# First batch of a pooled attention: values by probabilities of every second head in plain float32

## The chip, the cores and the metric

The kernel runs on one core of one Trainium2 chip. Its time is the device time of one execution in microseconds (us). Before the change the median of three runs is 1350.54 us (1350.36 to 1352.05). The profiled execution took 1351.29 us; the span of its instructions is 1349.5 us, so 1.79 us lie around the span.

## The reference, cut to what matters

An attention whose queries are averaged in pairs feeds a dense layer pair with a squared relu, and that feeds a gated layer pair. All is float32 (the weights of the first layers come as float64 words, decoded on the chip).

```python
B, H, S, D = 4, 8, 1152, 64
q_pool = q.reshape(B, H, S // 2, 2, D).mean(axis=3)          # 576 queries a head
scores = q_pool @ k.T / sqrt(D)
attn = exp(scores - max(scores)); attn = attn / (sum(attn) + 1e-9)
x = (attn @ v)                                                # 4 batches, 8 heads
x = x.transpose(0, 2, 1, 3).reshape(2304, 512)
h = x @ w_in; x = (s * relu(h) ** 2 + b) @ w_out              # 512 -> 2048 -> 512
y = (sigmoid(x @ w_gate) * (x @ w_val)) @ w_out2              # 512 -> 1536 -> 512
```

## The kernel before, in words

TensorE takes its operands in a rounded float32 here (`F32R`, fp32r in the profile's rows), one pass a matmul. Where the product must stay exact, an operand is split into a rounded high part and the rounded rest, and two or three matmuls are added in PSUM. A matmul of plain `F32` operands needs no split; the trace shows it as two matmul records.

The work is described as operations with an engine (or several to choose from), a duration, what they read and write, and the buffers they hold. `Plan.order` (line 1763) then plays the engines forward with these durations: on each engine the operation with the smallest key goes that is ready and whose buffers are free. The key is a due time (from the tables `ATTENTION` and `FEED`) plus a rank plus an offset by the operation's name from the table `MOVED`. Each engine then runs its list in that order and waits for semaphores only, so an instruction that waits holds everything behind it on its engine.

The four batches are staged. Batch 0's attention runs first, almost alone; from then on the attention of batch b+1 runs between the layers of batch b, and the layers of batch 3 end the kernel. Heads go in pairs (first head j=0, second head j=1), four pairs a batch. `pair_prep` (line 2378) loads and transposes q and k and loads v. For v of a split head it loads into `vn`, copies the high part and subtracts for the low part into `vt` (lines 2404 to 2406); for a head listed in `WHOLE` it loads straight into `vt`, as plain float32. Before, `WHOLE` holds heads 0 to 3 of batch 1.

Batch 0 is computed by rows (`pair_rows`, line 2635): queries on the partitions, so maxima and sums run along the free axis. `block` multiplies 128 queries by 1152 keys in three matmul groups (line 2657), DVE takes the maxima (2664), ACT the exponentials with their sums (2671). A middle block holds the last 64 queries of both heads. `group(j, g, ...)` (line 2688) then turns the probabilities back for the product with v. For g=0 it handles 256 queries and two chunks of 128 keys at a time (five units), for g=1 320 queries and one chunk at a time (nine units): 14 units a head, 56 for the four second heads, of which 36 have 320 columns, 16 have 512 and 4 have 256. One unit is:

1. transposes of the probabilities into a PSUM bank (2702, and 2704 for the middle block);
2. the split into `g`, two ways in turn: ACT copies PSUM to `pp` (2020), POOL or ACT rounds to the high part (2015 or 2013), POOL or DVE subtracts for the low part (2023); or ACT rounds from PSUM (2020) and DVE subtracts from PSUM (2026);
3. four or two matmuls of both parts by v's low and high columns (2724), adding into one bank.

At a group's end ACT copies that bank (`r o`) and DVE adds its two halves into `x` (2026, `x<-pp`). After a pair's last group the sums are inverted and `x` is scaled (2747 to 2773). Buffers: 8 PSUM banks in all, 4 of `g`, 6 of `pp`, 6 of `st`.

SP's queue loads q, k, v and the weights in one order. ACT, DVE and POOL decode the weights beside this (lines 2043 to 2063): 11 of the 68 decodes stand before 180 us.

Of the kernel before, what the change touches and what calls it, by code (L numbers as in the profile page):

```python
# [3018 lines left out]
```

## Time and profile before

| | us |
|---|---|
| median of 3 runs | 1350.54 |
| profiled execution | 1351.29 |
| its span | 1349.5 |
| PE busy | 1313.8 (97%) |
| PE weight loads busy | 1169.8 (87%) |
| DVE busy | 1128.4 (84%) |
| ACT busy | 903.6 (67%) |
| POOL busy | 903.2 (67%) |

PE is TensorE, DVE VectorE, ACT ScalarE, POOL GpSimd, SP the queue that starts DMAs. A matmul's record covers its whole way through the array, some 0.17 us more than the time until the next may start, so records overlap: a PE that starts few matmuls can still look busy. The spacing of starts is therefore taken from runs of equal matmuls in the timeline: in a row with n of them that spans T, and with t as the length of one, the spacing is (T - t) / (n - 1).

### The profile page before, as it was taken

To read this page: it belongs to the slowest core of one execution; us is meant where nothing else is said; L and a number is where in the kernel's file an instruction comes from. 1 tells how busy PE (TensorE), PEld (TensorE's weight loads), DVE (VectorE), ACT (ScalarE), POOL (GpSimd) and SP (SyncE) were. 2 spreads that over 40 slices of the span, in tenths; PEclk is the share of its full clock that TensorE was granted. 3 is DMA by queue.
4 is the path that set the end of the run, shared out by engine and by line. 5 is a ranking of instruction groups with operands and counts; after the bars stand their busy time and mean duration, and the time that the engine had idled before them with its cause. 6 is when DMAs were issued, how large, how long until landed. Compare 5 with 4: busy or idle time off the path is not lost.

```text
span 1349.5 us, 21795 instructions
## 1 busy us (share of the span) xinstructions
PE 1313.8 (97%) x7524; PEld 1169.8 (87%) x7524; DVE 1128.4 (84%) x1848; ACT 903.6 (67%) x1919; POOL 903.2 (67%) x767
## 2 busy tenths in 40 slices
PE   7999999998999999999999999999999999999998
PEld 6888888887888898888888888888888899999997
DVE  6899887998989998889989998898978646677675
ACT  6899977667888688768777667676855364343321
POOL 4578755657789876668868877586765455446562
PEclk9999999999999999999999999999999999999999
DMA  3246325876776764445343544343333434435332
GB/s 97 54 116 216 99 90 178 280 243 222 229 259 222 265 198 163 147 160 184 131 144 137 174 165 156 148 161 142 117 143 121 159 132 159 153 120 188 125 125 47
DMA packets 102373, 214.85 MB, mean 159 GB/s; under 512 B 49756, under 2 KB 72056, under 8 KB 86136
## 3 DMA queue, kind: packets, MB, share of 16 engines
q1 hardware_dynamic: 101096, 213.18, 47.4%
q8 instruction: 59, 0.97, 0.3%
q14 instruction: 50, 0.41, 0.1%
q10 hardware_dynamic: 1168, 0.29, 0.1%
HBM read 173.02 MB, written 40.43 MB: 158 GB/s over the span
## 4 chain that ended last, share of the span: by engine, by line
PE 78%; DVE 8%; ACT 6%; POOL 3%; DMA 3%; issue 2%; DVEq 0%; POOLq 0%; ACTq 0%
PE banks L2096 11%; PE banks L2098 11%; PE banks L2097 11%; PE banks L2493 6%; PE banks L2849 4%; PE banks L2851 4%; PE banks L2850 4%; PE banks L2567 3%; PE banks L2233 3%; PE banks L2235 3%; PE banks L2234 3%; PE banks L2559 2%; PE banks L2724 2%; PE banks L2549 2%; DVE st L2026 2%
## 5 line engine op out<-in xcount | busy, mean ns | idle before, releaser
L2026 DVE TENSOR_TENSOR st<-banks,st 128x288 f32<-128x288 f32 x384 | 171.9, 450 | 29.9 <-ACT st L2020 18.2
L2096 PE MATMUL banks<-xx,w 128*128 128x512 f32 x480 | 192.9, 402 | 0.9 <-DVE raw L2059 0.8
L2097 PE MATMUL banks<-xx,w 128*128 128x512 f32 x480 | 188.8, 393 | 0.0
L2098 PE MATMUL banks<-xx,w 128*128 128x512 f32 x480 | 188.8, 393 | 0.0
L2023 POOL TENSOR_TENSOR pp<-st,pp 128x864 fp32r<-128x864 f32 x76 | 173.3, 2285 | 12.2 <-ACT pp L2013 6.0
L2020 ACT COPY st<-banks 128x288 f32<-128x288 f32 x432 | 153.6, 407 | 40.8 <-PE banks L2493 29.9
L2493 PE MATMUL banks<-qT,kT 128*128 128x288 f32 x864 | 158.6, 303 | 2.5 <-DVE y L2340 1.1
L2026 DVE TENSOR_TENSOR st<-st,banks 128x864 f32<-128x864 f32 x144 | 148.2, 1043 | 4.3 <-PE banks L2467 3.9
L2493 PEld LDWEIGHTS banks<-qT,kT 128*128 128x128 f32 x864 | 134.3, 190 | 15.1 <-DVE st L2026 1.4
L2519 ACT ACTIVATE st<-st 128x864 f32<-128x864 f32 x144 | 132.7, 935 | 19.4 <-DVE st L2026 18.3
L2098 PEld LDWEIGHTS banks<-xx,w 128*128 128x128 f32 x480 | 90.5, 189 | 20.1
L2096 PEld LDWEIGHTS banks<-xx,w 128*128 128x128 f32 x480 | 90.7, 189 | 13.2 <-DVE raw L2059 1.0
L2097 PEld LDWEIGHTS banks<-xx,w 128*128 128x128 f32 x480 | 90.9, 189 | 10.8
L2013 ACT CAST pp<-st 128x864 fp32r<-128x864 f32 x102 | 93.4, 922 | 0.8 <-PE banks L2567 0.4
L2096 PE MATMUL banks<-g,w 128*128 128x512 f32 (+2 forms) x256 | 87.4, 342 | 0.0
L2097 PE MATMUL banks<-g,w 128*128 128x256 f32 (+1 forms) x256 | 86.5, 338 | 0.0
L2098 PE MATMUL banks<-g,w 128*128 128x512 f32 (+2 forms) x256 | 86.5, 338 | 0.0
L2023 POOL TENSOR_TENSOR g<-raw,g 128x512 fp32r<-128x512 f32 (+1 forms) x31 | 54.4, 1754 | 37.4 <-ACT g L2013 18.1
L2023 POOL TENSOR_TENSOR w<-raw,w 128x512 fp32r<-128x512 f32 x55 | 75.2, 1368 | 4.9 <-ACT w L2013 4.0
L2023 POOL TENSOR_TENSOR pp<-st,st 128x864 f32<-128x864 f32 x19 | 39.6, 2083 | 43.3 <-ACT st L2519 38.8
L2023 DVE TENSOR_TENSOR pp<-st,pp 128x864 fp32r<-128x864 f32 x44 | 65.6, 1490 | 2.9 <-PE banks L2559 1.1
L2567 PE MATMUL banks<-pp,vt 128*128 128x288 f32 x360 | 67.9, 297 | 0.0
(250 smaller groups left out, 3991.8 us busy)
## 6 DMA issues: line engine op xcount, KB each, us to landing
w<-d_2g_2v SPq DMA_DIRECT2D x26, 1024.0 KB
w<-d_1u_1u SPq DMA_DIRECT2D x24, 1024.0 KB
w<-d_1d_1d SPq DMA_DIRECT2D x24, 1024.0 KB
w<-d_2d_2d SPq DMA_DIRECT2D x18, 1024.0 KB
raw<-in_moe_w_out_dram SPq DMA_DIRECT2D x28, 512.0 KB
d_2g_2v<-w SPq DMA_DIRECT2D x12, 1024.0 KB
w<-d_2g_2v SPq DMA_DIRECT2D x20, 512.0 KB
qn<-in_q_dram SPq DMA_DIRECT2D x16, 576.0 KB
```

The lines of the kernel that those rows point to most:

```text
L2013: nc.scalar.copy(out=out(), in_=in_())
L2020: act(name, n, lambda: nc.scalar.copy(out=out(), in_=in_()), r, w, rank, sbuf=False)
L2023: shared(name, n, lambda e: ENGINE[e].tensor_tensor(out=out(), in0=in0(), in1=in1(), op=op), r, w, rank, 2.25)
L2026: dve(name, n, lambda: nc.vector.tensor_tensor(out=out(), in0=in0(), in1=in1(), op=op), r, w, rank)
L2096: nc.tensor.matmul(ps(), lhsT=whi(), rhs=xhi(), start=first, stop=False)
L2097: nc.tensor.matmul((ps_lo or ps)(), lhsT=whi(), rhs=xlo(), start=False, stop=False)
L2098: nc.tensor.matmul(ps(), lhsT=wlo(), rhs=xhi(), start=False, stop=last)
L2493: nc.tensor.matmul(ps.t[:, :HQ], lhsT=kT.t[:, c], rhs=qq[:, w, hf * HQ:(hf + 1) * HQ], start=(w == 0), stop=(w == 1))
L2519: act("exp", 3 * HQ, lambda s=s: nc.scalar.activation(out=s.t[:, :3], in_=s.t[:, :3], func=AF.Exp), [], parts, AT)
L2567: nc.tensor.matmul(acc.t[:, :HQ], lhsT=vt.t[:, 3 * i + c, cols], rhs=lo.t[:, c], start=False, stop=(i == c == 2))
L2849: nc.tensor.matmul(po.t, lhsT=hi, rhs=w.t[:, 0], start=(i == 0), stop=False)
L2850: nc.tensor.matmul(po.t, lhsT=hi, rhs=w.t[:, 1], start=False, stop=False)
```

## The change

Heads 1, 3, 5 and 7 of batch 0, the second head of each pair, are added to `WHOLE`. Their v is loaded straight into `vt` as plain float32, without the copy and the subtraction. In `group` their transposed probabilities are copied once from PSUM to a `pp` buffer, by ACT or DVE as the planner chooses, and are multiplied as plain float32 by v's 64 columns, into 64 rows of the bank. ACT copies these rows straight into `x`; the addition of two halves goes. First heads stay as they were. The two tables of due times and all of `MOVED` have other numbers, so the planner's order differs from the first operations on. Of the tables two lines stand here.

```diff
-WHOLE = [(1, h) for h in range(4)]
+WHOLE = [(0, h) for h in (1, 3, 5, 7)] + [(1, h) for h in range(4)]
-ATTENTION = (0.0, 158.683, 461.124, 811.569, 1195.188)
+ATTENTION = (0.0, 141.506, 451.626, 814.023, 1176.83)
...
             n = 256 + (64 if mid else 0)
+            whole = (0, 2 * hp + j) in WHOLE
...
-                t = g_slot()
+                t = slot("pp", "pp", [P, 3 * HQ]) if whole else g_slot()
...
+                if whole:
+                    def get(e, t=t, ps=ps, m=m):
+                        if e == "ACT":
+                            nc.scalar.copy(out=t.t[:, :m], in_=ps.t[:, :m])
+                        else:
+                            nc.vector.tensor_copy(out=t.t[:, :m], in_=ps.t[:, :m])
+
+                    plan.add("r p all", {"ACT": 50 + 0.833 * m, "DVE": 70 + 1.04 * m}, 0, get, [ps], [t], AT)
+
+                    def all_pv(cs=cs, t=t):
+                        for i, c in enumerate(cs):
+                            nc.tensor.matmul(acc.t[:D, :n], lhsT=vt[j].t[:, c, D:2 * D], rhs=t.t[:, i * n:(i + 1) * n],
+                                             start=(c == 0), stop=(c == NK - 1))
+
+                    pe("r pv all", len(cs) * mm(4 * n), all_pv, [t, (vt[j], 0)], [acc], AT)
+                    continue
...
+            if whole:
+                js = slice(j * D, (j + 1) * D)
+                copy_ps("r x all", n, lambda: xt()[js, g * 256:g * 256 + n], lambda: acc.t[:D, :n], [acc], [(x, hp, g, j)], AT)
+                return
```

By the two orders the whole program has: on PE 144 matmuls by split probabilities of second heads (72 of 256 columns, 72 of 320) before, 36 and 36 in plain float32 after; on ACT 28 casts and 36 copies out of PSUM fewer, 34 copies of whole probabilities and 8 copies into `x` more; on DVE 28 subtractions from PSUM and 8 additions into `x` fewer, 22 copies of whole probabilities more; on POOL 26 casts and 30 subtractions into `g` fewer. Of v's subtractions in the whole program POOL has 10 fewer and DVE 6 more.

On PE, at the end of batch 0's last pair (second head, 256 columns; `g` holds split probabilities, `xx` and `w` are the first layer's operands, `qT` and `kT` the next batch's), this stood before:

```order
L2096 MATMUL banks_95<-xx_273_1076,w_276_1271 128x512
L2097 MATMUL banks_95<-xx_273_1076,w_276_1271 128x512
L2098 MATMUL banks_95<-xx_273_1076,w_276_1271 128x512
L2724 MATMUL banks_95<-g_263_2251,vt1_112 128x256 x4
L2724 MATMUL banks_95<-g_265_2259,vt1_112 128x256 x4
L2724 MATMUL banks_95<-g_266_2291,vt1_112 128x256 x4
L2724 MATMUL banks_95<-g_268_2299,vt1_112 128x256 x2
L2493 MATMUL banks_95<-qT_239_2137,kT_241_2196 128x288 x8
```

In the changed kernel the same place on PE reads (`pp` holds whole probabilities; lines are those of the changed file, 62 to 83 higher):

```order
L2158 MATMUL banks_95<-xx_233_906,w_236_1134 128x512
L2159 MATMUL banks_95<-xx_233_906,w_236_1134 128x512
L2160 MATMUL banks_95<-xx_233_906,w_236_1134 128x512
L2783 MATMUL banks_95<-pp_225_2057,vt1_1420_218 64x256 x2
L2568 MATMUL banks_95<-ident_60,st_397_2103 96x128 x3
L2783 MATMUL banks_95<-pp_226_2071,vt1_1420_218 64x256 x2
L2529 MATMUL banks_95<-ident_60,mc_400_2176 128x96 x3
L2783 MATMUL banks_95<-pp_227_2090,vt1_1420_218 64x256 x2
L2783 MATMUL banks_95<-pp_228_2096,vt1_1420_218 64x256 x2
L2783 MATMUL banks_95<-pp_229_2118,vt1_1420_218 64x256
```

Fourteen matmuls became nine, each with one operand buffer and half the output rows, and transposes of the next batch's maxima now stand among them.

On ACT, in the same pair where the second head's units of 320 columns are made (`sg` holds maxima and sums, `st` the exponentials), this stood before:

```order
L2020 COPY pp_249_2122<-banks_95 128x320
L2020 CAST g_250_2113<-banks_95 128x320
L2671 ACTIVATE st_260_2066,sg_208_1694<-banks_95,sg_208_1694 128x384 x3
L2443 ACTIVATE qT_239_2137<-banks_95 128x256
L2443 ACTIVATE qT_240_2138<-banks_95 128x256
L2443 ACTIVATE qT_239_2137<-banks_95 128x256
L2671 ACTIVATE st_261_2119,sg_208_1694<-banks_95,sg_208_1694 128x384 x2
L2020 COPY pp_252_2182<-banks_95 128x320
L2020 CAST g_253_2178<-banks_95 128x320
```

In the changed kernel ACT has there:

```order
L2082 COPY pp_205_1949<-banks_95 128x320
L2775 COPY pp_214_1955<-banks_95 128x320
L2775 COPY pp_215_1961<-banks_95 128x320
L2775 COPY pp_216_1967<-banks_95 128x320
L2775 COPY pp_217_1972<-banks_95 128x320
L2775 COPY pp_218_1977<-banks_95 128x320
L2775 COPY pp_219_1982<-banks_95 128x320
L2733 ACTIVATE st_223_1937,sg_177_1638<-banks_95,sg_177_1638 128x384 x3
L2733 ACTIVATE st_224_1990,sg_177_1638<-banks_95,sg_177_1638 128x384 x3
L2505 ACTIVATE qT_208_2006<-banks_95 128x256
```

The copies and casts in turn became six copies in a row, which take six `pp` buffers, and the exponentials stand behind them.

## Rows read from the trace of the kernel before

**Rows 1.** Windows: length, busy PE, PEld, DVE, ACT, POOL, granted clock, DMA, GB/s
```profile
0.00:20.00 20.00, 12.04 (x51) 9.74 (x52) 12.71 (x30) 10.86 (x30) 7.20 (x15) 1.00 0.54 148
20.00:180.00 160.00, 149.95 (x1052) 136.35 (x1051) 141.70 (x320) 143.11 (x417) 115.30 (x145) 0.99 0.36 108
180.00:500.00 320.00, 312.53 (x1825) 273.13 (x1824) 288.90 (x530) 242.21 (x479) 231.63 (x226) 0.99 0.69 226
500.00:1000.00 500.00, 494.38 (x2740) 426.42 (x2739) 441.55 (x636) 363.71 (x731) 363.26 (x247) 1.00 0.44 150
```

**Rows 2.** Groups of PE's matmuls, 0 to 180 us
```profile
L2702 PE MATMUL banks<-ident,st 128*128 128x128 f32 x288 | 50.6, 282 | 3.2 <-DVE kT L2026 1.6 <-ACT pp L2020 0.6 <-DVE x L2026 0.4
L2657 PE MATMUL banks<-kT,qT 128*128 128x384 f32 x192 | 48.6, 369 | 3.3 <-DVE g L2026 1.0 <-DVE sg L2667 0.9 <-ACT st L2671 0.7
L2724 PE MATMUL banks<-g,vt 128*128 128x320 f32 x144 | 29.2, 322 | 1.8 <-DVE kT L2026 1.8
L2704 PE MATMUL banks<-ident,st 128*128 128x64 f32 x144 | 24.8, 255 | 0.0
L2724 PE MATMUL banks<-g,vt 128*128 128x256 f32 x144 | 22.3, 288 | 0.8 <-DVE g L2026 0.6 <-POOL g L2023 0.2
```

**Rows 3.** Timeline of PE: start, length, runs of equal matmuls
```profile
64.41 1.21 PE L2657 MATMUL banks<-kT,qT 128*128 128x384 f32 x6
...
130.03 1.04 PE L2702 MATMUL banks<-ident,st 128*128 128x128 f32 x8
...
146.78 1.10 PE L2724 MATMUL banks<-g,vt 128*128 128x256 f32 x8
...
163.20 1.42 PE L2724 MATMUL banks<-g,vt 128*128 128x320 f32 x8
...
200.11 1.62 PE L2549 MATMUL banks<-st,vt 128*128 128x288 f32 x6
...
645.14 0.39 PE L2096 MATMUL banks<-xx,w 128*128 128x512 f32 x1
645.37 0.40 PE L2097 MATMUL banks<-xx,w 128*128 128x512 f32 x1
```

**Rows 4.** The plain float32 matmuls of batch 1, as a group
```profile
L2549 PE MATMUL banks<-st,vt 128*128 128x288 f32 x144 | 38.5, 407 | 0.5 <-ACT st L2519 0.3
```

**Rows 5.** Groups of PE's matmuls, 500 to 1000 us
```profile
L2096 PE MATMUL banks<-xx,w 128*128 128x512 f32 x265 | 106.0, 400 | 0.0
...
L2493 PE MATMUL banks<-qT,kT 128*128 128x288 f32 x500 | 89.9, 298 | 0.1
L2096 PE MATMUL banks<-g,w 128*128 128x512 f32 x128 | 50.7, 396 | 0.0
...
...
L2567 PE MATMUL banks<-pp,vt 128*128 128x288 f32 x252 | 47.5, 297 | 0.0
```

**Rows 6.** Groups of ACT, DVE and POOL that make and split probabilities, 0 to 180 us
```profile
L2020 ACT COPY pp<-banks 128x320 f32<-128x320 f32 x44 | 18.8, 441 | 6.1 <-PE banks L2704 4.3 <-PE banks L2724 0.9 <-POOL xx L2023 0.6
...
L2026 DVE TENSOR_TENSOR g<-banks,g 128x320 fp32r<-128x320 f32 x36 | 17.4, 484 | 4.2 <-ACT g L2020 3.7
...
L2052 DVE TENSOR_SCALAR banks<-raw 128x512 uint32<-128x512 uint32 x11 | 7.4, 684 | 0.1
...
L2023 POOL TENSOR_TENSOR g<-pp,g 128x320 fp32r<-128x320 f32 x31 | 27.1, 876 | 3.1 <-ACT g L2013 1.2
...
L2015 POOL TENSOR_SCALAR g<-pp 128x320 fp32r<-128x320 f32 x33 | 16.0, 487 | 23.3 <-ACT pp L2020 20.8 <-issue 2.2
```

**Rows 7.** Waits of PE's queue for the split, 20 to 180 us: total, times, longest
```profile
PEld banks L2724 <- POOL g L2023: 3.1, 5, 2.0
...
PEld banks L2657 <- DVE g L2026: 1.6, 2, 1.1
```

**Rows 8.** Windows: a stretch at a lower granted clock
```profile
120.00:125.00 5.00, 3.21 (x23) 2.79 (x21) 4.59 (x10) 4.59 (x14) 4.75 (x7) 0.92 0.88 203
125.00:130.00 5.00, 5.00 (x34) 4.99 (x34) 4.23 (x14) 4.11 (x13) 4.10 (x7) 0.74 0.56 150
```

More of the change, by code (lines that the diff above doesn't have):

```diff
@@ new lines @@
+    "g lo :1": -624.213,
+    "g lo :1 1": -587.005,
+    "g lo :1 2": -736.919,
+    "g lo :1 3": -317.86,
+    "w load :1": 8.74,
+    "w load :1 1": -22.206,
+    "w load :1 2": 16.638,
+    "w load :1 3": 38.371,
+    "w top :1": -110.713,
+    "w top :1 0": -131.577,
+    "w top :1 1": -164.894,
+    "w top :1 2": -245.257,
+    "w scale :1": 96.148,
+    "w scale :1 0": -3.73,
+    "w scale :1 1": -235.138,
+    "w scale :1 3": 75.471,
+    "w low :1": 19.303,
+    "w low :1 0": 22.056,
+    "w low :1 1": -3.699,
@@ new lines @@
+    "w keep :1 1": 869.269,
+    "w keep :1 3": 498.251,
+    "ff down :1": -600.214,
+    "ff down :1 0": -465.814,
+    "ff down :1 1": -107.207,
+    "ff down :1 3": -53.711,
+    "ff y add :1": 146.753,
+    "ff y add :1 0": 29.181,
+    "ff y add :1 2": 190.059,
+    "ff y add :1 3": 171.806,
+    "column sum :1": 57.83,
+    "column sum :1 1": 53.611,
+    "column sum :1 2": 41.358,
+    "column sum :1 3": 37.225,
+    "bias :1": 17.433,
+    "bias :1 3": 21.995,
+    "y bias :1": -0.85,
@@ new lines @@
+    "h lo :1": -158.518,
+    "h lo :1 0": -133.518,
+    "h lo :1 2": -124.896,
+    "h lo :1 3": -90.807,
+    "w load :2": -24.975,
+    "w load :2 1": -22.925,
+    "w load :2 2": 58.903,
+    "w load :2 3": 22.318,
+    "w top :2": 80.612,
+    "w top :2 0": 134.907,
+    "w top :2 1": 218.068,
+    "w top :2 3": 201.198,
+    "w scale :2": 41.411,
+    "w scale :2 1": -148.93,
+    "w scale :2 2": 181.077,
+    "w scale :2 3": -219.6,
+    "w low :2": -40.146,
+    "w low :2 0": -1.826,
+    "w low :2 2": 97.295,
@@ new lines @@
+    "down 2 :2": -168.386,
+    "down 2 :2 0": 10.346,
+    "down 2 :2 1": -6.571,
+    "down 2 :2 2": -187.646,
+    "out :2": -8.384,
+    "out :2 0": -8.138,
+    "w load :3": 168.825,
+    "w load :3 0": -36.531,
+    "w load :3 2": -253.414,
+    "w load :3 3": -59.871,
+    "w top :3": 48.639,
+    "w top :3 1": 29.343,
+    "w top :3 2": 45.677,
+    "w top :3 3": 160.293,
+    "w scale :3": 24.221,
+    "w scale :3 0": -87.852,
+    "w scale :3 2": -188.209,
+    "w scale :3 3": -157.584,
@@ L926 @@
+    "w lo :3 1": -68.671,
+    "w lo :3 2": -34.004,
+    "w keep :3": 369.214,
+    "w keep :3 0": 114.032,
+    "w keep :3 2": 149.92,
+    "w keep :3 3": 390.672,
+    "down 2 :3": 9.803,
+    "down 2 :3 0": 15.338,
+    "down 2 :3 2": -311.876,
+    "down 2 :3 3": -109.951,
+    "out add :3": 10.34,
+    "out add :3 1": -33.597,
+    "out add :3 2": 26.511,
+    "out add :3 3": -12.594,
+    "p2 xx up :3": 281.512,
+    "p2 xx up :3 0": -97.163,
     "p2 xx up :3 1": 3.827,
     "p2 xx up :3 2": 21.574,
-    "gate :3": 0.463,
@@ new lines @@
+    "out store :3 0": 41.464,
+    "out store :3 3": 52.021,
+    "qk @0": 40.127,
+    "qk @0 1": -21.099,
+    "qk @0 2": -184.437,
+    "qk @0 3": -23.193,
+    "s copy @0": 8.959,
+    "s max @0": -16.368,
+    "s max @0 0": -188.17,
+    "s max @0 1": -65.497,
+    "s max @0 3": -159.561,
+    "max T @0": -192.521,
+    "max T @0 0": 174.768,
+    "max T @0 1": -148.037,
+    "max T @0 2": -259.244,
+    "max @0": -80.712,
+    "max @0 1": 86.267,
+    "max @0 2": -151.52,
+    "max @0 3": 89.838,
@@ L1669 @@
[L1669 to L1683 removed]
+    "qk @1 2": -28.613,
+    "s copy @1": 120.385,
+    "s copy @1 0": 127.998,
+    "s copy @1 1": -4.138,
@@ new lines @@
+    "s copy @1 2": 6.364,
+    "s max @1": 121.767,
+    "s max @1 0": -101.619,
+    "s max @1 1": 31.012,
+    "s max @1 3": -98.237,
+    "max T @1": -63.755,
+    "max T @1 0": 239.184,
+    "max T @1 2": -43.605,
+    "max T @1 3": -130.542,
+    "max @1": 210.27,
+    "max @1 0": 506.456,
+    "max @1 1": 58.353,
+    "max @1 3": 433.273,
+    "max rows @1": -351.52,
+    "max rows @1 1": -178.99,
+    "max rows @1 2": -636.598,
+    "max rows @1 3": -913.163,
+    "s - max @1": 184.599,
@@ new lines @@
+    "s - max @1 1": 620.011,
+    "s - max @1 2": 199.794,
+    "s - max @1 3": 471.631,
+    "exp @1": 776.939,
+    "exp @1 1": 320.705,
+    "exp @1 2": 692.83,
+    "exp @1 3": 662.865,
+    "pv whole @1": 3.899,
+    "pv whole @1 0": 43.739,
+    "pv whole @1 2": -187.488,
+    "pv whole @1 3": -60.627,
+    "sums @1": -14.447,
+    "sums @1 1": -16.459,
+    "sums @1 3": -12.914,
+    "x @1": 16.622,
+    "x @1 0": -33.843,
+    "x @1 2": -44.603,
+    "x @1 3": -20.148,
+    "sums out @1": -45.981,
@@ new lines @@
+    "qk @3 1": -18.925,
+    "qk @3 2": -20.672,
+    "s copy @3": 185.616,
+    "s copy @3 0": -17.68,
+    "s copy @3 1": 22.231,
+    "s copy @3 2": 13.996,
+    "s max @3": -105.437,
+    "s max @3 0": -81.914,
+    "s max @3 1": 58.588,
+    "s max @3 3": -153.681,
+    "max T @3": -209.929,
+    "max T @3 0": 167.066,
+    "max T @3 1": -449.527,
+    "max T @3 3": -270.095,
+    "max @3": 185.726,
+    "max @3 0": 636.758,
+    "max @3 1": -38.346,
+    "max @3 3": 52.347,
+    "max rows @3": -206.994,
@@ new lines @@
+    "W whole :0 2": 94.598,
+    "T :0": -138.639,
+    "T :0 0": -42.904,
+    "T :0 1": -6.118,
+    "T :0 2": -185.319,
+    "T hi :0": -64.726,
+    "T hi :0 0": -42.028,
+    "T hi :0 1": -51.013,
+    "T hi :0 3": -174.535,
+    "T lo :0": -104.467,
+    "T lo :0 1": -41.899,
+    "T lo :0 2": -8.069,
+    "T lo :0 3": -190.338,
+    "ff B11 :0": -324.026,
+    "ff B11 :0 1": 30.958,
+    "ff B11 :0 2": -73.555,
+    "ff B11 :0 3": -91.592,
+    "ff first :0": 116.928,
+    "ff first :0 0": 115.025,
@@ new lines @@
+    "ff first :0 1": 147.057,
+    "ff first :0 2": 114.901,
+    "ff B21 :0": 1.537,
+    "ff B21 :0 1": 6.874,
+    "ff B21 :0 2": -9.635,
+    "ff sum :0": 56.28,
+    "ff sum :0 0": 140.984,
+    "ff sum :0 1": -43.588,
+    "ff sum :0 3": -121.057,
+    "ff T2 :0": -6.432,
+    "ff T2 :0 0": 2.73,
+    "ff T2 :0 1": 15.28,
+    "ff T3 :0": 129.013,
+    "ff T3 :0 1": -12.458,
+    "ff T3 :0 2": 1.182,
+    "ff T3 :0 3": -3.906,
+    "ff T1 :0": -232.69,
+    "ff T1 :0 0": -22.045,
+    "ff T1 :0 2": 59.462,
@@ new lines @@
+    "T hi :1 1": -63.623,
+    "T hi :1 3": -28.537,
+    "T lo :1": -8.219,
+    "T lo :1 1": 18.364,
+    "T lo :1 2": 39.4,
+    "T lo :1 3": -2.489,
+    "ff B11 :1": 59.047,
+    "ff B11 :1 0": -92.935,
+    "ff B11 :1 2": -179.601,
+    "ff B11 :1 3": -44.011,
+    "ff first :1": -124.656,
+    "ff first :1 0": -29.186,
+    "ff first :1 2": -106.684,
+    "ff B21 :1": -6.226,
+    "ff B21 :1 0": -243.865,
+    "ff B21 :1 1": 266.78,
+    "ff B21 :1 3": -136.039,
+    "ff sum :1": -0.361,
@@ new lines @@
+    "p2 yy up :2": -8.946,
+    "p2 yy up :2 0": 3.521,
+    "p2 yy up :2 2": -36.376,
+    "p2 yy up :2 3": 6.841,
+    "w fetch half :2": 152.976,
+    "w fetch half :2 0": 62.714,
+    "w fetch half :2 2": 49.076,
+    "w fetch half :2 3": 36.2,
+    "W whole :2": 8.657,
+    "W whole :2 0": 12.261,
+    "W whole :2 2": 23.104,
+    "W whole :2 3": 24.027,
+    "T :2": 11.539,
+    "T :2 0": 43.356,
+    "T :2 1": 17.758,
+    "T :2 2": 75.039,
+    "T hi :2": -126.17,
+    "T hi :2 1": -76.122,
@@ new lines @@
+    "p2 B22 :2 1": -3.966,
+    "p2 B22 :2 2": -59.609,
+    "p2 B22 :2 3": 0.917,
+    "w fetch half :3": -34.138,
+    "w fetch half :3 3": -56.471,
+    "W whole :3": -146.044,
+    "W whole :3 0": -36.372,
+    "W whole :3 1": -82.563,
+    "W whole :3 2": -73.665,
+    "T :3": 113.224,
+    "T :3 0": 182.314,
+    "T :3 1": 106.707,
+    "T :3 3": 93.283,
+    "T hi :3": 14.634,
+    "T lo :3": -63.79,
+    "T lo :3 0": -169.7,
+    "T lo :3 2": -42.968,
+    "T lo :3 3": -92.861,
+    "p2 B11 :3": 26.063,
@@ new lines @@
+    "p2 B11 :3 0": -2.227,
+    "p2 B11 :3 2": -169.531,
+    "p2 B11 :3 3": -109.677,
+    "p2 first :3": 6.382,
+    "p2 first :3 0": -7.627,
+    "p2 first :3 2": -24.913,
+    "p2 B21 :3": 40.279,
+    "p2 B21 :3 0": 54.855,
+    "p2 B21 :3 1": 89.639,
+    "p2 B21 :3 3": 19.198,
+    "p2 sum :3": 1.531,
+    "p2 T2 :3": 25.492,
+    "p2 T2 :3 0": 61.285,
+    "p2 T2 :3 2": 107.917,
+    "p2 T2 :3 3": 50.546,
+    "p2 T3 :3": -24.195,
+    "p2 T3 :3 1": 20.122,
+    "p2 T3 :3 2": 2.001,
+    "p2 T3 :3 3": 3.615,
```

1645 lines of the change are left out of this document (680 added, 965 removed), and 1402 rows, old and new, of the table MOVED.

## The prediction, made blind

> **What bounds the kernel now.** I read the windows first, with one cut where batch 0's attention ends, then PE's groups and its timeline, then the groups of the other engines and the waits. In the windows the reader is to see two regimes [rows 1]. From 500 to 1000 us PE is busy 494 of 500 us (98.9%), DVE 88%, ACT and POOL 73%. From 20 to 180 us, batch 0's attention, PE is busy 150 of 160 us (94%), DVE 141.7 (88.6%), ACT 143.1 (89.4%) and POOL 115.3 (72%). Records of matmuls overlap, so I weigh PE by spacing. Runs of equal matmuls give (1.21 - 0.369) / 5 = 0.168 us for 384 columns, (1.04 - 0.282) / 7 = 0.108 for a transpose, (1.10 - 0.288) / 7 = 0.116 for 256 columns, (1.42 - 0.322) / 7 = 0.157 for 320, and 0.23 between the starts of two of 512 [rows 2, 3]. A plain float32 matmul of 288 columns is two records, each (1.62 - 0.407) / 5 = 0.243 [rows 3, 4].
>
> Up to 180 us PE issues 1103 matmuls (51 in the first 20 us and 1052 in the 160 behind them [rows 1]). By groups: 288 x 0.108 = 31.1, 192 x 0.168 = 32.3, 144 x 0.157 = 22.6, 144 x 0.116 = 16.7; the 144 records of 64 columns scaled from the plain float32 ones, 0.243 x 64 / 288 = 0.054, give 7.8 [rows 2]. The other 191, transposes and 384-column ones, I put at 0.13 (between 0.108 and 0.168), 25 us. The sum is 135; less 51 x 0.13 = 7 in the first 20 us, 129 us of work stand in the 160 us stretch: 81%. The same reckoning from 500 to 1000 us: 3 x (265 + 128) matmuls of 512 columns at 0.23 are 271, 500 + 2 x 252 of 288 columns (two groups of 252, one shown) at 0.137 (between 256 and 320) are 137, and 557 others at about 0.15 are 84: 492 of 500, 98% [rows 1, 5]. So in batch 0's attention PE has about 31 us to spare while DVE and ACT are as full as they get anywhere; later PE itself is the bound.
>
> **The change part by part.** *PE, added.* Second heads have 72 matmuls of 256 and 72 of 320 columns, half of the two groups [rows 2]: 72 x 0.116 + 72 x 0.157 = 19.7 us go. In come 36 + 36 plain float32 ones, two records each: 72 x 0.243 x 256 / 288 + 72 x 0.243 x 320 / 288 = 15.6 + 19.4 = 35.0. Net +15.3 us of PE work, all before about 180 us. That the new ones fill only 64 output rows no row prices; from below it could save half of 35, from above nothing. I take nothing, since columns alone set the spacing of every row here.
>
> *ACT.* 28 casts and 36 copies go, 34 + 8 copies come: 22 fewer x 0.441 = 9.7 us less [rows 6], 143 becomes 133.
>
> *DVE.* 28 subtractions from PSUM go, 28 x 0.484 = 13.6; 8 additions go, at the same 0.484 about 3.9; 22 copies from PSUM come. No row shows this copy; the subtraction of the same 320 columns from PSUM (0.484) bounds it near by, the 512-column operation (0.684) from above, and nothing below about 0.4 is likely. I take 0.484, 10.6 us; at 0.684 it would be 15.0. If all 6 v subtractions that DVE has more (576 columns, so at least 0.684) fall here, 4.1. Net between -7 and +1.6; I take -4 us [rows 6].
>
> *POOL.* 26 roundings x 0.487 and 30 subtractions x 0.876 into `g` go: 39 us less [rows 6].
>
> *Waits.* PE's named waits for the split are 3.1 + 1.6 = 4.7 us for both heads, so some 2.4 go [rows 7]. A new hold comes: a whole unit keeps its `pp` buffer until PE has multiplied it (2 x 0.27 = 0.54 us for 320 columns), and six copies in a row on ACT take all six. The next copy would then wait for PE, and behind it on ACT stand exponentials, which the next transposes wait for. POOL needs the same buffers for first heads. The load of a second head's v now waits on SP until PE has left that `vt` buffer, with weight loads queued behind. I cost it at nothing, as the next pair's first head (its matmuls by v alone are 9.8 us / 2 = 4.9 us by the terms above) stands between; without that cover each of three pairs would wait for one load.
>
> *What it comes to.* PE's work in the stretch becomes 129 + 15.3 = 144 us. The stretch ends unchanged if PE is filled to 144 / 160 = 90%. If DVE stays at 88.6%, its 4 us less are worth 4 / 0.886 = 4.5 us; ACT (133 of 155, 86%) and POOL no longer bind. PE would have to be filled to 144 / 155.5 = 92.6%, above the 81% of now and under the 98% seen later with DVE equally full. I take 5 us off, since ACT's 10 us less also frees DVE of its waits. Behind the stretch PE has the same work as before and hardly a gap, so the end moves by what the stretch's end moves. The sum against the profiled execution: 1349.5 + 1.8 - 5 = 1346.3; it lies 0.75 above the median, so 1345.5.
>
> A rule speaks against this. The trace over the whole span has PE's weight loads as the busiest record there is to judge PE by, 87% against DVE's 84%; in this stretch the order is turned, 136.35 of 160 (85%) against 88.6% and 89.4% [rows 1]. The Trainium skill ("Perfetto Trace Analysis", Identifying the Most-Contended Engine) says to judge TensorE by its weight loads, not by its matmuls, and to spare the fullest engine first. Taken over the span, that rule makes all 15.3 us arrive at the end, which is rival D; taken by regime, which the page also asks for, it agrees with the sum above.
>
> From 125 to 130 us the granted clock was 0.74 of 2.4 GHz, part of it at 1.2 GHz, after 5 us in which PE was busy only 3.21 [rows 8]. The Trainium skill ("TensorE: Matmul & The Clock Gate", What's actually happening) has activity hold the gate open and idleness close it. By it a fuller PE would get back up to 0.08 x 5 + 0.26 x 5 = 1.7 us here and the sum would be 1343.8; I leave it out, since the dip can as well move.
>
> **The rivals.**
> *A, slower: buffers held by PE.* Place: second heads' copies on ACT and DVE, above. Most of PE's idle time before its groups is put down to k's low parts, maxima and exponentials [rows 2], which the change does not touch, so the gaps may stay gaps and PE's new work come on top. It decides when PE's fill stays under 90%. At 87%, about midway between 81% and the 92.6% that I count on, the stretch is 144 / 0.87 = 166 us, 6 longer: 1356.5. Against it: fewer steps lie between transposes and products, and banks come free after one copy instead of two readers.
> *B, no change: given back.* From 180 to 500 us DVE is 90% busy and DMA 0.69 [rows 1], with 57 of 68 decodes still to come. Layers that could start 5 us sooner then wait for weights, and the end stands: 1350.5. For it: that stretch is the fullest for DMA. Against: the decodes' engines lose work too.
> *C, much faster.* ACT, DVE and POOL together lose some 53 us; PE fills to 98% as later: 144 / 0.98 = 147 us, 13 shorter, 1337.5. Against it: the chain from scores to products still crosses three engines in each block.
> *D, slower by all of it.* PE bounds everywhere, and 15.3 us arrive: 1365.8. For it: PE's 94% in the stretch; against: 31 us of spacing unfilled there.
>
> **How the numbers follow.** What a measurement here can tell from no change is about 0.2%, 2.7 us. Forecast 0.38 (1341 to 1348 is its own range, from a DVE copy of 0.4 to 0.684 us and a fill of 91 to 95%), C 0.16, B 0.22, A 0.16, D 0.08. Faster is forecast and C, 0.54; the same is B, 0.22; slower is A and D, 0.24. The range from 1336 to 1359 leaves out D, a little of A and a little of C, some 0.17.
>
> **What would show it.** Right: line 2783's records have a spacing of 0.21 to 0.22 and 0.27; PE's last work of batch 0's attention, just before 180 us so far, comes at about 175; DVE stays near 88% up to there, ACT falls to 86%, POOL under 55%. Wrong: ACT or DVE copies of line 2775 and 2777 that wait for PE (A); the same early end, but the first layers' matmuls idle on weights (B); PE work over 98% up to 170 us and an end before 170 (C); an end of the stretch after 190 us (D). If second records start closer than 0.2 us, plain float32 is cheaper than batch 1's rows say and the gain is larger.

## The result, and the profile after

The changed kernel takes 1363.88 us (median of 4 runs, 1361.23 to 1364.63) against 1350.45 for the kernel before in the same comparison: a ratio of 1.0093, 95% interval 1.007 to 1.0116. It is slower by about 12.6 us; the forecast was 1345.5, 5 us faster. The profiled execution of the changed kernel took 1361.23 us with a span of 1359.4, 9.9 us more than the span before.

The windows of the changed kernel, with the columns of [rows 1], and one cut more at 200 us:

```profile
0.00:20.00 20.00, 13.03 (x53) 10.60 (x54) 13.29 (x32) 10.31 (x30) 6.47 (x15) 1.00 0.60 162
20.00:180.00 160.00, 156.22 (x995) 124.91 (x993) 128.88 (x295) 125.59 (x370) 71.03 (x89) 1.00 0.33 102
20.00:192.00 172.00, 168.22 (x1058) 132.91 (x1056) 138.13 (x312) 132.44 (x387) 71.66 (x90) 1.00 0.32 99
180.00:200.00 20.00, 20.00 (x112) 14.98 (x111) 14.63 (x28) 12.45 (x31) 2.54 (x3) 1.00 0.20 45
500.00:1000.00 500.00, 494.77 (x2760) 428.41 (x2761) 451.39 (x647) 365.14 (x732) 365.89 (x248) 1.00 0.44 148
```

The transposes of batch 0's inverted sums, which close a pair, start at 58.3, 96.9, 141.5 and 179.8 us before and at 56.4, 100.3, 145.2 and 191.9 after. So batch 0's attention ends 12.1 us later, and the row from 20 to 192 us is the one to lay beside 20 to 180 in [rows 1]: PE is busy 98% of it instead of 94%, while DVE (80%), ACT (77%) and POOL (42%) have fallen from 89, 89 and 72%. From 500 us on PE is as full as before.

PE's groups from 0 to 192 us, with the columns of [rows 2] (line 2783 is the new plain float32 product, 2803 the split one):

```profile
L2719 PE MATMUL banks<-kT,qT 128*128 128x384 f32 x192 | 46.7, 367 | 0.3 <-ACT st L2733 0.2
L2783 PE MATMUL banks<-pp,vt 128*64 128x320 f32 x72 | 24.7, 450 | 0.0
...
L2783 PE MATMUL banks<-pp,vt 128*64 128x256 f32 x72 | 17.3, 385 | 0.0
L2803 PE MATMUL banks<-g,vt 128*128 128x320 f32 x72 | 15.2, 324 | 0.4 <-POOL g L2085 0.4
L2803 PE MATMUL banks<-g,vt 128*128 128x256 f32 x72 | 10.5, 283 | 0.0
```

Before, PE idled 3.3 us ahead of the score matmuls [rows 2]; now it is 0.3. PE is nearly never seen idle, and a busy share can no longer tell what it loses. The timeline of PE at two places, with the columns of [rows 3], does:

```profile
56.95 1.58 PE L2719 MATMUL banks<-kT,qT 128*128 128x384 f32 x6
58.46 4.10 PE L2783 MATMUL banks<-pp,vt 128*64 128x256 f32 x18
62.49 0.80 PE L2719 MATMUL banks<-kT,qm 128*128 128x384 f32 x3
...
85.42 1.34 PE L2719 MATMUL banks<-kT,qT 128*128 128x384 f32 x6
86.69 1.29 PE L2783 MATMUL banks<-pp,vt 128*64 128x320 f32 x4
87.91 0.44 PE L2765 MATMUL banks<-ident,st 128*128 128x128 f32 x2
```

From the second record of a run of equal matmuls on, the spacing is as forecast: 0.216 us for 256 columns and 0.269 for 320 in the median. At the ends of a run it isn't. The four records of the second one above start at 86.69, 87.01, 87.27 and 87.54, so the first gap is 0.320 us; the transpose follows at 87.91, 0.363 us later instead of 0.269. About 95 ns are lost on entering line 2783, some 50 on its first record and again about 95 on leaving it, and no row calls that idle. Only the weight loads' waits hint at it (same columns as [rows 7], 20 to 192 us):

```profile
PEld banks L2783 <- issue: 3.7, 19, 0.3
PEld banks L2765 <- issue: 2.5, 5, 0.5
```

The granted clock's fall at 120 to 130 us [rows 8] is absent in this execution, with a fuller PE:

```profile
120.00:125.00 5.00, 4.65 (x37) 4.34 (x36) 4.02 (x10) 4.42 (x13) 3.33 (x5) 1.00 0.71 281
125.00:130.00 5.00, 5.00 (x32) 3.33 (x31) 4.58 (x11) 4.04 (x12) 3.49 (x5) 1.00 0.42 116
```

That does not hold for the kernel as such. The profiled execution has a mean granted clock of 0.999 over its span; the three others of the changed kernel have 0.995 to 0.996 and take 2.5 to 3.4 us longer. Where the clock fell in them no trace shows. So some of the 12.6 us can be clock: at 0.998 to 0.999 the kernel with 128 rows below is 7.6 us ahead by the spans, against 8.5 by the ratios.

### The profile page after: what moved, and what is told of

Read it like the earlier page. It is cut to its first block, busy times and chain, and to the rows that moved or that the text cites. A ratio compares the mean times of both kernels' runs of the same rounds, so it can differ in the third digit from the quotient of the medians.

```text
span 1359.4 us, 21680 instructions
## 1 busy us (share of the span) xinstructions
PE 1329.3 (98%) x7524; PEld 1162.6 (86%) x7524; DVE 1130.8 (83%) x1833; ACT 895.7 (66%) x1895; POOL 859.7 (63%) x706
## 5 line engine op out<-in xcount | busy, mean ns | idle before, releaser
L2088 DVE TENSOR_TENSOR st<-banks,st 128x288 f32<-128x288 f32 x384 | 171.5, 449 | 24.6 <-ACT st L2082 14.2
L2085 POOL TENSOR_TENSOR pp<-st,pp 128x864 fp32r<-128x864 f32 x71 | 158.4, 2237 | 13.3 <-ACT pp L2075 7.8
L2075 ACT CAST pp<-st 128x864 fp32r<-128x864 f32 x107 | 98.0, 921 | 0.7 <-PE banks L2629 0.4
L2085 POOL TENSOR_TENSOR pp<-st,st 128x864 f32<-128x864 f32 x24 | 50.6, 2108 | 67.4 <-ACT st L2581 46.6
L2085 DVE TENSOR_TENSOR pp<-st,pp 128x864 fp32r<-128x864 f32 x49 | 78.6, 1605 | 8.5 <-ACT pp L2075 6.1
L2733 ACT ACTIVATE st<-banks,sg 128x384 f32<-128x384 f32 x108 | 62.7, 601 | 17.1 <-DVE sg L2729 16.6
```

What stands on the lines that cost most here:

```text
L2075: nc.scalar.copy(out=out(), in_=in_())
L2085: shared(name, n, lambda e: ENGINE[e].tensor_tensor(out=out(), in0=in0(), in1=in1(), op=op), r, w, rank, 2.25)
L2088: dve(name, n, lambda: nc.vector.tensor_tensor(out=out(), in0=in0(), in1=in1(), op=op), r, w, rank)
L2733: act("r exp", 384 + 224, lambda c=c, ps=ps: nc.scalar.activation(out=p.t[:, c * 384:(c + 1) * 384], in_=ps.t[:, :384], func=AF.Exp, bias= ...
```

## The experiments

Theory 1, made after the result: PE, not ACT and DVE, sets the stretch once it gets more work; the plain float32 columns (15.3 us) and the switches to and from the 64-row matmuls (about 7) arrive, less what fits into gaps. Rivals: that copies wait for `pp` buffers which PE holds; that the re-tuned tables cost the time; and the prediction's own, that ACT and DVE are the bound. Differences in us below are (ratio - 1) x 1350.5, with the interval of the ratio.

### The 64 output rows

`e3_cols128`:

```diff
-nc.tensor.matmul(acc.t[:D, :n], lhsT=vt[j].t[:, c, D:2 * D], rhs=t.t[:, i * n:(i + 1) * n],
+nc.tensor.matmul(acc.t[:, :n], lhsT=vt[j].t[:, c, D:], rhs=t.t[:, i * n:(i + 1) * n],
```

> The changed kernel with one thing altered: the plain float32 products of the second heads take v's 64 columns and the 64 columns of ones beside them as weights, so that all 128 output rows are filled, as batch 1's plain float32 products do. The order on every engine is that of the changed kernel. Theory 1 (TensorE bounds batch 0's attention, and 64-row plain float32 matmuls pay some 95 ns at each switch to or from another kind, about 7 us in sum): 1355 to 1359 us. Rival (TensorE waits for buffers that whole probabilities hold, or for a chain through ACT and DVE): no change against the changed kernel's 1363.9, 1362 to 1366. Rival (the re-tuned tables cost the time): the same, 1362 to 1366.

Measured: ratio 1.003 (1.0018 to 1.0041), +4.1 us against before, so 8.5 us better than the change; the spans, 1351.8 and 1359.4, differ by 7.6. The same places in its timeline:

```profile
55.17 1.58 PE L2719 MATMUL banks<-kT,qT 128*128 128x384 f32 x6
56.60 4.05 PE L2783 MATMUL banks<-pp,vt 128*128 128x256 f32 x18
60.29 0.88 PE L2719 MATMUL banks<-kT,qm 128*128 128x384 f32 x3
...
83.73 0.86 PE L2719 MATMUL banks<-kT,qT 128*128 128x384 f32 x4
84.43 1.24 PE L2783 MATMUL banks<-pp,vt 128*128 128x320 f32 x4
85.50 0.38 PE L2765 MATMUL banks<-ident,st 128*128 128x128 f32 x2
```

Two products (four records) now take 85.50 - 84.43 = 1.07 us up to the next kind, against 87.91 - 86.69 = 1.22. From the records of both traces, 20 to 192 us (median ns between two starts):

```
switch                                   64 rows   128 rows   times
scores (384 columns) -> line 2783            268        172      10
transpose (128 columns) -> line 2783         202        109       6
transpose (64 columns) -> line 2783          205        112       6
line 2783, 320 columns -> transpose          363        269      15
line 2783, 320 columns -> q, k transpose     363        269       5
line 2783, 320 columns, first -> second      320        272      25
line 2783, 256 columns, first -> second      267        219       8
transposes behind line 2783, first -> second 165        109      15
```

Each switch costs 93 to 96 ns with 64 rows. Two more gaps grow, by about 50 to 55 ns each: behind the first record of a run, and behind the first record of the kind that follows. The gaps between are the same in both kernels. From the last record before a run to the second record behind it, 64 rows cost 291 ns in the median of 33 runs, 8.5 us in their sum. Batch 0's attention, with the same columns in the same order, ends at 184.9 us instead of 191.9: 7.0 of the 7.6 us are there.

`e5_pe_64` and `e5_pe_128` do the same in the kernel before, with its order and its splits untouched:

```diff
-                    for w in range(2):
+                    for w in range(j, 2):      # once for second heads
                         for i, c in enumerate(cs):
+                            if j:      # e5_pe_128: acc.t[:, :n] and columns :2 * D
+                                nc.tensor.matmul(acc.t[:D, :n], lhsT=vt[j].t[:, c, D:2 * D].bitcast(F32),
+                                                 rhs=part(t, 1)[:, i * n:(i + 1) * n].bitcast(F32), ...)
+                                continue
 ...   # e5_pe_64 also: the copy and the addition at a group's end read the 64 rows
```

> The kernel before, with its order, its tables and its splits as they were, but each second head's chunk multiplied once in plain float32 with 64 output rows (of the low part alone, so x of these heads is wrong) instead of twice in one pass: only TensorE's side of the change. Theory 1 (TensorE bounds here already): 15.3 us of columns and up to 7 us of switches arrive less a few us of gaps, 1364 to 1373 us. The prediction's theory (31 us to spare on TensorE beside full ACT and DVE): hidden, 1350 to 1355. Rival (tables): about the kernel before, 1350 to 1355.

> As the run with TensorE's side of the change alone (order, tables, splits of the kernel before; each second head's chunk multiplied once, in plain float32, by the low part; x of these heads is wrong), but with all 128 output rows filled: the added columns (15.3 us) without the switches of 64 rows. Theory 1, now with a threshold (TensorE has some 10 us to spare, since 9.9 us less work moved nothing, and beyond that each us arrives): 15.3 - 10 = 5 us slower than before, 1353 to 1357. Rival (every us of added TensorE work arrives): 1361 to 1366. The prediction's theory (31 us to spare): 1349 to 1352.

Measured: 1.011 (1.0096 to 1.0124), +14.9 us, with 64 rows; 1.0053 (1.0039 to 1.0067), +7.2, with 128. Their spans, 1362.3 and 1354.7, again differ by 7.6; a run of 64 rows costs 292 ns more in the median of 25. So PE's side alone is enough for the whole loss of the change, and the price of the 64 rows is shown in two orders.

### Tables and buffers

`e4_relief` keeps the change's order and tables but gives PE its old work back:

```diff
-nc.tensor.matmul(acc.t[:D, :n], lhsT=vt[j].t[:, c, D:2 * D], rhs=..., start=(c == 0), ...)
+for w in range(2):   # pp rounded, a constant as weights
+    nc.tensor.matmul(acc.t[:, :n], lhsT=cw.to_broadcast([P, P]), rhs=..., start=(c == 0 and w == 0), ...)
```

> The changed kernel, with the second heads' products given back their former cost on TensorE: the probabilities are copied once as before, but rounded, and multiplied twice in one pass each by a constant 128-column weight, so x of these heads is not the product with v. ACT, DVE and POOL stay relieved as in the change; order and tables are the changed kernel's. Theory 1 (the added TensorE work is the whole loss): not slower than the kernel before, 1343 to 1351 us. Rival (the tables cost the time, not the arithmetic): 1360 to 1365. Rival (pp buffers held until TensorE has multiplied them): part of the loss stays, since a unit is still held 0.32 us instead of 0.54: 1355 to 1360.

Measured: 1.0022 (1.0012 to 1.0032), +3.0: 9.6 us of the change's 12.6 go with PE's work alone. The rest was missed by theory 1: with all the relief and PE as before, this is still not faster than before. `e9_full_oldorder` below, the change's arithmetic with 128 rows in the old order, has +5.0 against +4.1 for `e3_cols128` in the new: for that arithmetic the new tables are no loss. With the relief alone they are one: `e8_relief_oldorder` below has -3.0 in the old order against +3.0 here, though this run takes more work from the other engines. So the rest belongs, as far as these runs tell, to an order made for other operations. Three runs meant to part tables from arithmetic let the planner order anew with the old tables:

```diff
 # e1_128_oldtables: e3_cols128    e4b_relief_oldtables: e4_relief, product planned as 2 * mm(n)
 # e6a_half_old: e3_cols128 with heads (3, 7) in place of (1, 3, 5, 7)
-ATTENTION = (0.0, 141.506, ...)   # FEED and MOVED likewise
+ATTENTION = (0.0, 158.683, ...)
```

> The changed kernel with 128 output rows, and with the due times and offsets of the kernel before in place of its own. Theory 1 (arithmetic costs the time, the tables only fit it to the order): not faster than the same with the new tables (1354.0), 1353 to 1362. Rival (the new tables cost several us): faster, 1345 to 1350.

> The relief of ACT, DVE and POOL alone, as before with a constant 128-column weight in two passes (x of the second heads is not the product with v), but with the tables of the kernel before and with the planner's duration for these products set to that of two passes, so that the order is not laid out for slow products. The prediction's theory (ACT and DVE bound batch 0's attention, TensorE has room): 5 to 13 us faster, 1337 to 1346. Rival (neither alone bounds it; the chain from scores to products and TensorE's order do): within 3 us of before, 1348 to 1353.

> Half the dose: only heads 3 and 7 of batch 0 in plain float32, with 128 output rows, tables of the kernel before. TensorE gets 7.7 us more, ACT, DVE and POOL about half of the relief. Threshold theory (some 10 us of TensorE work fit into the gaps): no slower than before, 1346 to 1351. Rival (added work arrives in proportion, 3.8 us for the whole dose): 1351 to 1354. Rival (each us arrives): 1357.

Measured: 1.022, 1.0178 and 1.0142, 19 to 30 us slower. All three missed what either theory expected: the old tables fit one set of operations, and these three got a poor order with them (in the first, the second pair takes 62.2 us instead of 38.7). They tell nothing of the arithmetic; from here on every kernel keeps the order of before, instruction by instruction.

### What bounded the stretch before

`e7_less_pe`, less for PE alone:

```diff
-                    for w in range(2):
+                    for w in range(j, 2):
```

> The kernel before, with the second heads' high products left out (72 matmuls of 256 and 72 of 320 columns, half of what they multiply; x of these heads is only the low part's product): 9.9 us less work for TensorE by spacing, everything else and the order unchanged. Theory 1 (TensorE bounds batch 0's attention): 6 to 10 us faster, 1340 to 1345 us. The prediction's theory (ACT and DVE bound it, TensorE has 31 us to spare): within 2 us of the kernel before, 1348 to 1352.

Measured: 0.9997 (0.9985 to 1.0009), no change. Theory 1 as first stated falls for the kernel before: there PE is not the bound. What is left out is the high part's product; the low part's, which waits for the subtraction, stays. In the profile the 9.9 us came back as waits and as a lower clock (its waits of PE's queue, then its windows):

```profile
PEld banks L2724 <- POOL g L2023: 6.3, 11, 2.0
```

```profile
40.00:45.00 5.00, 3.51 (x19) 3.11 (x20) 4.47 (x9) 4.20 (x12) 0.51 (x2) 0.74 0.56 121
45.00:50.00 5.00, 4.95 (x39) 4.67 (x39) 3.54 (x10) 4.80 (x16) 1.75 (x3) 0.92 0.04 6
...
120.00:125.00 5.00, 2.71 (x19) 2.20 (x18) 4.61 (x10) 4.86 (x14) 4.67 (x8) 0.93 0.86 216
125.00:130.00 5.00, 5.00 (x26) 4.96 (x26) 4.23 (x14) 3.84 (x12) 4.09 (x7) 0.50 0.52 138
130.00:135.00 5.00, 4.91 (x30) 4.01 (x29) 4.86 (x10) 4.12 (x10) 3.77 (x4) 0.89 0.84 300
```

The wait for POOL's split was 3.1 us [rows 7] and is 6.3. The clock misses 0.26 + 0.08 + 0.07 + 0.50 + 0.11 of five us each, 5.1 us, where before it missed 1.7 [rows 8]. Over all executions the difference is smaller: the clock of the whole span is 0.9965 here in the mean of 11 and 0.9984 for the kernel before in the mean of 20 beside them, some 2.5 us of 1350.

`e8_relief_oldorder` and `e11_dve_relief` relieve the others and leave PE its work:

```diff
 # units of second heads, one copy in place of the split; PE multiplies the high part twice
+act("r p", ..., nc.scalar.copy(out=part(t, 0)[:, :m], in_=ps.t[:, :m]))           # first way, both
+dve("r pT lo", ..., nc.vector.tensor_copy(out=part(t, 0)[:, :m], in_=ps.t[:, :m])) # second way, e8
+act("r pT hi", ..., nc.scalar.copy(out=part(t, 0)[:, :m], in_=ps.t[:, :m]))        # second way, e11
```

> The relief alone at the order of the kernel before, kept instruction by instruction: the second heads' probabilities are rounded out of PSUM once (by ACT or by DVE in turn), the other copy, the rounding and both kinds of subtraction are left out, and TensorE multiplies the high part twice, so it does the same work as before (x of these heads lacks the low parts). ACT loses about 12 us, POOL about 42, DVE's subtractions become copies. The prediction's theory (ACT and DVE bound batch 0's attention, TensorE is free 31 us): 5 to 13 us faster, 1337 to 1345. Two limits side by side (TensorE with its chain as near as ACT and DVE): within 4 us of before, 1346 to 1351.

> The relief at the order of the kernel before with DVE's part in place of ACT's: every unit of a second head is rounded out of PSUM once by ACT, DVE's 28 subtractions (13.6 us) and POOL's work on these heads are left out, ACT keeps its amount, TensorE multiplies the high part twice (x of these heads lacks the low parts). If DVE bounds batch 0's attention: 6 to 13 us faster than before, 1337 to 1344. If several engines in turn bound it (relief of ACT and POOL gave 1348.1): within 4 us of before, 1346 to 1350.

Measured: 0.9978 (0.9966 to 0.999), -3.0 us, and 0.997 (0.9958 to 0.9981), -4.1. Row 20 to 180 us of e8, then of e11:

```profile
20.00:180.00 160.00, 150.37 (x1067) 136.68 (x1066) 141.29 (x321) 131.35 (x386) 80.43 (x99) 1.00 0.37 110
```

```profile
20.00:180.00 160.00, 150.70 (x1067) 138.06 (x1066) 130.27 (x293) 141.19 (x414) 80.16 (x99) 0.99 0.36 110
```

Against [rows 1], e8 frees ACT of 11.8 us and POOL of 35, e11 frees DVE of 11.4 and POOL of 35. Neither brings more than 4.1 us: even if all of that were DVE's doing, a us less of its work is worth 0.36 us of time, not 1 / 0.886 = 1.13.

`e10_both` and `e14_dve_and_pe` are these two with one product a chunk:

```diff
-                    for w in range(2):
+                    for w in range(2 - easy):     # easy: second heads of batch 0
```

> The relief at the order of the kernel before, and in addition only one product a chunk (the high part by both parts of v; x of the second heads lacks the low part of the probabilities): TensorE has 9.9 us less, ACT 12 and POOL 42 less. Two limits side by side: only both together pay, 6 to 12 us faster than before, 1338 to 1344, though less TensorE work alone gave nothing (1349.8). If ACT and DVE alone bound: the same as the relief alone, within 2 us of that run. If the order or another chain bounds: within 3 us of before.

> The order of the kernel before; each unit of a second head is rounded out of PSUM once by ACT, and multiplied once, by the low and high parts of v: DVE loses 28 subtractions (13.6 us), POOL its work on these heads, TensorE 9.9 us (x of the second heads lacks the low part of the probabilities). If DVE and TensorE are limits side by side: 8 to 13 us faster than before, 1337 to 1342. If the chain from scores through ACT to products holds the stretch: no faster than with DVE relieved alone (1346.2), 1344 to 1348; if the granted clock falls more often with the emptier TensorE, up to 3 us of it are given back.

Measured: 0.9989 (0.9977 to 1.0002), -1.5 us, and 0.9959 (0.9941 to 0.9977), -5.5; the second is the fastest of all kernels here, but with the shortened product. Theory 1, by now "two limits side by side", misses both: the intervals of e10 and e8, and of e14 and e11, overlap. Row and largest waits of PE's queue in e14:

```profile
20.00:180.00 160.00, 145.59 (x986) 131.47 (x984) 130.57 (x292) 140.37 (x412) 79.89 (x98) 0.96 0.36 110
```

```profile
PEld banks L2703 <- DVE kT L2026: 4.2, 3, 2.0
PEld banks L2657 <- ACT st L2671: 3.4, 7, 1.1
```

PE now waits for banks that DVE's split of the next pair's k and ACT's exponentials still read (in the kernel before 2.3 and 1.2 us in that view), and its clock is down to 0.96 over 160 us. In the order of before no single engine holds the stretch. That steps which hand over to each other hold it is argued, not shown, and which chain of them stays open. ACT and DVE were relieved together in the new order alone (`e4_relief`), so that these two bound it side by side is not ruled out.

### The dose

`e9_full_oldorder` and `e12_full_act` are the whole change with 128 rows in the old order, with e8's and e11's copies; `e13_third_pair` (head 5, ACT's copies) and `e13_half` (heads 3 and 7, e8's copies) are parts of it:

```diff
+nc.tensor.matmul(acc.t[:, :n], lhsT=vt[j].t[:, c, D:].bitcast(F32),        # e13: :2 * D, v split
+                 rhs=part(t, 0)[:, i * n:(i + 1) * n].bitcast(F32), start=(c == 0), stop=(c == NK - 1))
```

> The whole change's arithmetic with 128 output rows at the order of the kernel before: as the run before it, but unrounded, with v copied unrounded and one plain float32 product a chunk; the reference's result is computed. TensorE gets the 15.3 us of columns, the relief as there. Threshold theory with no worth of the relief: 1353 to 1358, as TensorE's side alone with 128 rows (1356.6). If the relief makes room: 1344 to 1350. The prediction's theory: 1340 to 1346.

> As the whole arithmetic at the order of before (plain float32, 128 output rows, the reference's result), with every unit copied by ACT, so that DVE loses its 28 subtractions instead of ACT its casts. If TensorE bounds once its 15.3 us are added: as with the other relief, 1354 to 1358. If DVE was what kept TensorE's gaps open: 1343 to 1350.

> Only head 5 of batch 0 in plain float32 probabilities, at the order of before: copied once by ACT, multiplied by the low and high parts of v side by side (128 output rows, parts added as before; the reference's result). 3.8 us more TensorE work, in the pair that has its largest gaps, its only fall of the granted clock (1.7 us) and a DVE that is 96 to 98% busy. Threshold theory: hidden, and the clock may come back: 1347 to 1350. In proportion (5.5 of 15.3): 1351 to 1352.

> Heads 3 and 7 of batch 0 in the same way, at the order of before, with the copies by ACT and DVE in turn: 7.7 us more TensorE work, half of the relief. Threshold theory (some 10 us fit): 1348 to 1351. In proportion: 1352 to 1353. Each us arrives: 1357.

Measured, with what PE gets by spacing:

```
kernel            PE work   relief        time against before (interval)
e7_less_pe           -9.9   none          -0.4 (-2.0 to +1.2)
e13_third_pair       +3.8   head 5         0.1 (-1.2 to +1.4)
e13_half             +7.7   heads 3, 7    +6.1 (+3.9 to +8.2)
e5_pe_128           +15.3   none          +7.2 (+5.3 to +9.0)
e9_full_oldorder    +15.3   ACT, POOL     +5.0 (+3.1 to +7.0)
e12_full_act        +15.3   DVE, POOL     +7.0 (+4.7 to +9.2)
e3_cols128          +15.3   all, new order +4.1 (+2.4 to +5.5)
```

15.3 us of columns cost 4 to 7 us, whoever is relieved, so 8 to 11 fit in. They don't fit evenly: head 5's 3.8 us vanish in the pair with the largest gaps, heads 3 and 7 pay 3.9 to 8.2 us for their 7.7, against the threshold theory's 1348 to 1351. Part of that can be clock: the six executions go from 1353.8 us at a mean clock of 1.000 to 1359.1 at 0.995. In the profile the clock fell where it did not before, in the first pair, whose instructions and their order are the same in both:

```profile
40.00:45.00 5.00, 3.66 (x24) 3.16 (x24) 4.47 (x9) 4.35 (x14) 0.98 (x3) 0.85 0.53 121
45.00:50.00 5.00, 5.00 (x35) 4.94 (x35) 3.04 (x9) 3.73 (x13) 1.26 (x2) 0.81 0.00 0
```

In the kernel before:

```profile
40.00:45.00 5.00, 3.66 (x29) 3.12 (x27) 4.66 (x11) 4.81 (x14) 0.99 (x3) 1.00 0.59 121
45.00:50.00 5.00, 5.00 (x42) 4.92 (x41) 4.20 (x13) 4.74 (x16) 1.42 (x4) 1.00 0.10 20
```

0.15 + 0.19 of five us each are 1.7 us; the edit begins behind this pair, so they are not its work. Such falls come and go between executions of one kernel too: the executions of the kernel before have mean clocks from 0.995 to 1.000.

## Why the prediction was wrong

*The work, right.* Spacing 0.21 to 0.22 and 0.27 (0.216 and 0.269, but for the first gap of a run); ACT -9.7, DVE -4, POOL -39 against -10.7, -3.6 and -43.6 (143.1 to 132.4, 141.7 to 138.1, 115.3 to 71.7 up to the stretch's end). DVE's copy, which no row showed, was taken at 0.484 and is 0.483 us, as the groups of DVE and ACT in the changed kernel, 20 to 180 us, show:

```profile
L2777 DVE COPY pp<-banks 128x320 f32<-128x320 f32 x17 | 7.6, 483 | 2.4 <-PE banks L2767 2.2
```

```profile
L2775 ACT COPY pp<-banks 128x320 f32<-128x320 f32 x19 | 7.8, 430 | 4.1 <-PE banks L2767 2.9 <-issue 0.7 <-DVE banks L2117 0.3
```

(columns as in [rows 6]; the second row is ACT's copy).

*The 64 rows, wrong by 8 us.* "I take nothing, since columns alone set the spacing of every row here." Every row read was a run of equal matmuls, and inside a run that holds. What 64 rows cost stands at its ends, 291 ns a run: 7.6 us of span in two orders, 8.5 and 7.7 by the ratios. "From above nothing" was no bound. The trace before could mislead, since it has one-pass matmuls of 64 rows between others, at 0.13 us either way:

```profile
367.79 0.29 PE L2562 MATMUL banks<-pp,vt 128*64 128x288 f32 x1
367.92 0.29 PE L2561 MATMUL banks<-pp,vt 128*128 128x288 f32 x1
368.05 0.29 PE L2562 MATMUL banks<-pp,vt 128*64 128x288 f32 x1
```

The Trainium skill ("TensorEngine Tiling (Array Packing)", Key Properties) says that a change of the tiling mode drains TensorE, and under Available Configurations it lists 128x64 apart from 128x128. The stops of 93 to 96 ns agree, the one-pass rows do not; which instructions change the mode no run here shows. The sentence should have been a rival with a price.

*The fill, wrong by 9.4 us.* "PE would have to be filled to 144 / 155.5 = 92.6%." With 128 rows PE's 144 us took until 184.9 us, 144 / 164.9 = 87%. That is rival A's figure, but not by A's buffers: the copies of lines 2775 and 2777 wait for transposes (line 2767 in the two rows above), not for products to free a buffer. The 31 us to spare were counted right, but they are not room that can be filled. From the records, 20 to 180 us, the time between starts beyond the spacing of equal matmuls (a lower clock included; by the spacing that is taken, the middle column can be 1 to 3 us lower and the work as much higher):

```
kernel         work    in gaps under 120 ns    over 120 ns
before        126.9         15.6 (1006)         17.6 (44)
after         134.4         16.7 (963)           8.8 (29)
e3_cols128    139.8         10.6 (1004)          9.7 (29)
e5_pe_128     133.9         12.0 (963)          14.3 (38)
e7_less_pe    117.0         17.4 (904)          25.6 (68)
```

Nearly half of it stood in a thousand stops of less than 120 ns, as between score matmuls or at each change from the 64-column transposes to the next (54 ns in the median). Neither kind went away, as the other half of A has it (the gaps may stay gaps): under the added work the short stops gave up 5.0 us and the 44 longer gaps 7.9 in the new order, 3.6 and 3.3 in the old. What keeps the rest open no run shows.

*The worth of the relief, wrong.* "If DVE stays at 88.6%, its 4 us less are worth 4 / 0.886 = 4.5 us." Taking 11.4 us from DVE gave 4.1 with PE as before, and next to nothing once PE had the new work (+7.0 with DVE relieved, +7.2 without). A busy share near 90% did not make DVE the bound.

*Behind the stretch, right.* The end moved by 9.9 us where the stretch's end moved by 12.1; in `e5_pe_64`, with the old order, a lag of 13.7 us where batch 1 begins (182 us before) is still 13.0 near the last batch's end of attention (1011 us).

*The rivals.* D gave 1365.8 and marked itself by an end after 190 us. Both came near or true, by luck: its reason (PE bounds everywhere, all 15.3 us arrive) did not. 4 to 7 of 15.3 arrive, and 8 that it didn't know of. B (no change) and C (a much shorter stretch) did not come. The Trainium skill's rule to judge TensorE by its weight loads ("Perfetto Trace Analysis", Identifying the Most-Contended Engine) names PE as the bound over the span; `e7_less_pe`, with no gain from 9.9 us less, speaks against that for this stretch of the kernel before. The Trainium skill's rule on the clock ("TensorE: Matmul & The Clock Gate", What's actually happening) agrees in part. The three kernels with 9.9 us less PE work in the old order have mean clocks of 0.9965, 0.9958 and 0.9956 against 0.998 of the kernel before beside them, `e5_pe_128` with 15.3 us more has 0.9993; but the changed kernel, its PE as full, has 0.9962 in the mean of four executions.

The stretch was forecast to end at 175.5 and ended at 191.9 us: 9.4 us are the fill (184.9 with 128 rows), 7.0 the 64 rows. Behind the stretch 2.2 of these 16.4 us were made up (its end moved by 12.1, the kernel's by 9.9), which leaves 14.2 of the 18.4 us between forecast and result. Of the rest, 0.7 is a forecast gain of 5 us from a stretch 4.3 us shorter, and 2.7 and 0.8 us are by what the profiled executions lie below and above their kernels' medians. No experiment beats both kernels with the whole product; the change with 128 rows is 8.5 us better than the change and 4.1 behind the kernel before.

## What to carry to other kernels

Spare time of an engine beside its work is not room: of 31 us counted here, new work of 15.3 us found 8 to 11, and neither the short stops nor the long gaps closed. Try the added work alone at a fixed order before counting on it. Read the spacing at the ends of runs too, and give a shape that no row shows a price from above that isn't zero. A busy share near 90% on three engines names no bound; take one piece of work away at a fixed order and see. And the same relief can be worth 6 us more in one order than in another.
